# Turning the normalized x by transposing DMAs instead of TensorE, in an attention and spectral kernel

## The chip, the cores and the metric

The kernel runs on one core of a Trainium2 chip. The metric is the time of one execution in device microseconds (us); of several executions the median is given.

## The reference, cut to what matters

Two layers, each an attention block and a spectral filter, both on a layernorm of x and both added to x. S is 2048 tokens, D is 1024 columns, there are 32 heads of 32 columns.

```python
def _A_ref(x, wqkv, wo):                      # attention
    qkv = (x @ wqkv).reshape(B, S, 3, H, Dh).transpose(2, 0, 3, 1, 4)
    q, k, v = qkv[0], qkv[1], qkv[2]
    p = softmax(einsum("bhqd,bhkd->bhqk", q, k) * Dh ** -0.5)
    return einsum("bhqk,bhkd->bhqd", p, v).transpose(0, 2, 1, 3).reshape(B, S, D) @ wo
def _B_ref(x, w_r, w_i):                      # spectral filter
    return irfft2(rfft2(x) * (w_r + 1j * w_i))

x = x + _A_ref(layernorm(x), wqkv, wo)
x = x + _B_ref(layernorm(x), w_r, w_i)
...                                           # the same two lines once more
```

## The kernel before

The tokens are cut into 16 tiles of 128, the chunks of a query or key sum have 512 tokens (four tiles, `NCH` = 4), and the heads go in 8 groups of four (`NG`). x stays in on-chip memory (`ap.x`). The products with the weights are done in float16 pairs: a number is split into a high float16 part (ScalarE, ACT in the profile) and a low one, the rest (VectorE, DVE), by `split` (L167, L168); three matmuls, high by high, high by low and low by high, make one product.

Each layer's attention begins with a **prologue**, which makes everything that the first group of heads needs:

- `ln_tile(t)` normalizes a token tile: two statistics on DVE (`bn_stats`, L111, L112; in layer 1 half of those of the first six tiles are made earlier), small instructions on DVE and one on GpSimd (L119 to L124, L302), then one ACT instruction that writes the normalized tile `xn` in float32 (L304). In layer 0 it also starts the load of the x tile four places on (L293).
- `tr_tile(t, xn)` turns it, so that columns lie on partitions: eight TensorE transposes with an identity matrix into PSUM (L310), and then `split` from PSUM into `xh` and `xl`, views of the big buffer (named big in the profile).
- `v_tiles(ph, t2)` makes V for two token tiles, 48 matmuls of 256 columns (L372), eight times.
- `qk_chunk(ph, c)` makes a chunk of K or Q, 24 matmuls of 512 columns (L328), four times for K and four times for Q. Its split goes to ACT and DVE, and its squares to GpSimd (L332), for `norms` and `mkbias` (L345 to L358), which yield the bias of the first Exp.
- `prep` loads a weight piece by SP and splits it (L248 to L258); in layer 1 this was done earlier, beside the spectral stage.

`xn` comes from a pool with the tag "p", which has eight slots of 4 KB a partition. The attention's K, Q and V are written over x tiles that have been normalized (R in the profile is that buffer).

Behind the prologue comes the main loop over groups, query chunks and key tiles (scores L548, Exp L552, sums with V L558, row sums L571), whose TensorE and ACT order is written out by hand, with the weights' products of later groups put between. In the prologue no order is written out: there the framework orders the instructions of each engine, by the place in the program and by its own estimates of when an operand is ready. It also places all semaphores. Each engine and each DMA queue then works its list in order. Nearly all DMAs are issued by SP, one queue.

Between the two attentions stands the spectral stage of layer 0. At its end the sixteen tiles of the new x are stored to memory by SP (L982, 512 KB each), in the program ahead of layer 1's prologue.

Of the kernel before, what the change touches and what calls it, by code (L numbers as in the profile page):

```python
# [6 lines left out]
F32 = mybir.dt.float32  # L7
F32R = mybir.dt.float32r
F16 = mybir.dt.float16
# [91 lines left out]
SX = 2.0 ** 8  # L101
# [7 lines left out]
def bn_stats(nc, sm, x):  # L109
    st = sm.tile([128, 2, 6], F32, name="st")  # L110
    nc.vector.bn_stats(st[:, 0], x[:, 0:512])  # L111
    nc.vector.bn_stats(st[:, 1], x[:, 512:1024])  # L112
    return st
# [14 lines left out]
def ln_stats(nc, sm, cst, st, mv):  # L128

    nc.vector.bn_aggr(mv, st)  # L130
    return ln_scale(nc, sm, cst, mv, nc.vector)
# [33 lines left out]
def split(nc, hi, lo, src, scale):  # L165

    nc.scalar.activation(hi, src, AF.Copy, scale=scale)  # L167
    nc.vector.scalar_tensor_tensor(lo, src, scale, hi, op0=ALU.mult, op1=ALU.subtract)  # L168


def run(g):
    for _ in g:
        pass
# [52 lines left out]
class Weights:  # L226
# [5 lines left out]
    def prep(self, ph):  # L232
        nc, ap, wp = self.nc, self.ap, self.wp
        kind, g = ph
        if kind == "v":
            w = self.W[ph] = ap.wvp.tile([128, 2, 8, 256], F16, name="wv")
            sl = [(w[:, 0, 4 * j:4 * j + 4, 128 * i:128 * i + 128], w[:, 1, 4 * j:4 * j + 4, 128 * i:128 * i + 128],
                   wp[g + i, 2, :, 512 * j:512 * j + 512]) for i in range(2) for j in range(2)]
        else:
            w = self.W[ph] = ap.wqp.tile([128, 2, 8, 128], F16, name="wqk")  # L240
            sl = [(w[:, 0, 4 * j:4 * j + 4], w[:, 1, 4 * j:4 * j + 4],
                   wp[g, 0 if kind == "q" else 1, :, 512 * j:512 * j + 512]) for j in range(2)]
        st = []

        def load():
            if len(st) < len(sl):
                s = ap.sgp.tile([128, 4, 128], F32, name="wst")
                nc.sync.dma_start(s, sl[len(st)][2].rearrange("p (d c) -> p d c", c=128))  # L248
                st.append(s)
        for _ in range(3):  # L250
            load()
        yield
        for i, (h, l, _) in enumerate(sl):
            split(nc, h, l, st[i], SW)
            if self.flag is not None:
                wm = ap.sm.tile([128, 1], F32, name="wm")
                nc.vector.tensor_reduce(wm, st[i], axis=AX.XY, op=ALU.max, apply_absolute_value=True)
                nc.vector.tensor_max(self.flag, self.flag, wm)  # L258
            load()
            yield  # L260
# [3 lines left out]
PH0 = [("v", 0), ("k", 0), ("q", 0)]  # L264


def attention(nc, tc, layer, ap, xin, yd, wts, wo, cst, dram, flags):

    ident = cst["ident"]
    W, prep = wts.W, wts.prep  # L270
    od = dram.tile([2, NG, 128, 2048], F16, name=f"od{layer}")
    small, psum = ap.small, Pools(tc, None)
    pp, qp, sgp, wqp, wvp = ap.pp, ap.qp, ap.sgp, ap.wqp, ap.wvp
    sq, on, on2, sm = ap.sq, ap.on, ap.on2, ap.sm
    psS = psum("at_psS", 3, space=PSUM)
# [4 lines left out]
    def bank():  # L280

        if both:
            both.append(True)
            if len(both) % 2:
                return psO.tile([128, 512], F32, name="o")
        return psX.tile([128, 512], F32, name="x")
    xhl = ap.big.bitcast(F16).rearrange("p (c a d n) -> p c a d n", a=2, d=8, n=512)
    xh, xl = ([xhl[:, c, a] for c in range(4)] for a in range(2))
    V, K, Q, bias, nrm, mx = {}, {}, {}, {}, {}, {}

    def ln_tile(t):
        if layer == 0 and t + 4 < 16:
            nc.sync.dma_start(ap.x[:, t + 4], xin[(t + 4) * 128:(t + 5) * 128, :])  # L293
        mv = flags["mv"][:, layer * 16 + t]
        if layer and t < NST:
            st = flags["st"][:, t]
            nc.vector.bn_stats(st[:, 1], ap.x[:, t, 512:1024])
        else:
            st = bn_stats(nc, sm, ap.x[:, t])
        r = ln_stats(nc, sm, cst, st, mv)  # L300
        b = sm.tile([128, 1], F32, name="b")
        nc.vector.scalar_tensor_tensor(b, mv[:, 0:1], -1.0, r, op0=ALU.mult, op1=ALU.mult)  # L302
        xn = pp.tile([128, 1024], F32, name="xn", tag="p")
        nc.scalar.activation(xn, ap.x[:, t], AF.Identity, bias=b, scale=r)  # L304
        return xn

    def tr_tile(t, xn):
        pt = psS.tile([128, 8, 128], F32, name="s")
        for d in range(8):
            nc.tensor.transpose(pt[:, d], xn[:, d * 128:(d + 1) * 128], ident)  # L310
        c, o = t // 4, (t % 4) * 128
        split(nc, xh[c][:, :, o:o + 128], xl[c][:, :, o:o + 128], pt, SX)

    def qk_chunk(ph, c):
        kind, g = ph
        w = W[ph]
        if c == 0:
            if kind == "k":
                K[g] = ap.k[g % 3]
            else:  # L320
                Q[g] = qp.tile([128, 2, 2048], F16, name="Q") if g % 2 else ap.q
            p_, n_ = (qp, "Q") if ph == ("q", 0) else (sq, "sq")
            nrm[ph] = p_.tile([128, 4, 512], BF16, name="sq", tag=n_)
        t = (K if kind == "k" else Q)[g][:, :, c * 512:c * 512 + 512]
        ps = bank()
        for d in range(8):
            for i, (a, b) in enumerate(((w[:, 0, d], xh[c][:, d]), (w[:, 0, d], xl[c][:, d]), (w[:, 1, d], xh[c][:, d]))):
                nc.tensor.matmul(ps, a, b, start=d == 0 and i == 0, stop=d == 7 and i == 2)  # L328
                if d < 7 or i < 2:
                    yield  # L330
        split(nc, t[:, 0], t[:, 1], ps, SQ / (SX * SW))
        nc.gpsimd.tensor_tensor(nrm[ph][:, c], t[:, 0], t[:, 0], op=ALU.mult)  # L332
        if c == 3:
            left_norms.append(ph)
        yield
# [3 lines left out]
    def norms():  # L339
        kind, g = ph = left_norms.pop(0)  # L340
        if g not in mx:
            mx[g] = sm.tile([128, 2], F32, name="mqk")
        ps = psS.tile([128, 2, 512], F32, name="s")
        for c in range(4):
            nc.tensor.matmul(ps[32 * c:32 * c + 32, 0], cst["bones"], nrm[ph][:, c], start=True, stop=True)  # L345
        i = 0 if kind == "k" else 1
        nc.vector.reduce_max(mx[g][:, i:i + 1], ps[:, 0], axis=AX.X)
        if kind == "q":
            mkbias(g)

    def mkbias(g):
        r = sm.tile([128, 2], F32, name="mall")
        nc.gpsimd.partition_all_reduce(r, mx[g], 128, bass.bass_isa.ReduceOp.max)
        b = sm.tile([128, 1], F32, name="bpr")
        nc.gpsimd.tensor_tensor(b, r[:, 0:1], r[:, 1:2], op=ALU.mult)
        nc.gpsimd.tensor_tensor(b, b, cst["half"], op=ALU.pow)
        bias[g] = sm.tile([128, 1], F32, name="bias")
        nc.gpsimd.tensor_scalar(bias[g], b, -SCALE / (SQ * SQ), None, op0=ALU.mult)  # L358
# [142 lines left out]


    vk = [v_tiles(PH0[0], t) for t in range(8)]
    xn = [ln_tile(0), ln_tile(1)]
    if not layer:
        run(prep(PH0[0]))

    def ln_to(t):
        while len(xn) <= min(t, 15):
            xn.append(ln_tile(len(xn)))  # L510
    for t in range(4):
        tr_tile(t, xn[t])
        ln_to(t + 2)
        if not layer and t in (1, 2):
            run(prep(PH0[t]))
        if t % 2:
            run(vk.pop(0))
    ln_to(7)
    for c in range(NCH):
        t = 4 * c + 4  # L520
        run(qk_chunk(PH0[1], c))
        if t < 16:
            tr_tile(t, xn[t])
            ln_to(t + 3)
        run(qk_chunk(PH0[2], c))
        if t < 16:
            for i in range(1, 4):
                tr_tile(t + i, xn[t + i])
                ln_to(t + i + 3)
                if i == 2:  # L530
                    run(vk.pop(0))
        elif c == 3:
            norms()
            norms()
    for v in vk:
        run(v)
    both.clear()
# [77 lines left out]
    with tc.manual_schedule(engines={mybir.EngineType.PE, mybir.EngineType.Activation}):  # L615
        for g in range(NG):
# [3 lines left out]
            for u in range(NCH * NKT):  # L620
                c, kt = divmod(u, NKT)
# [25 lines left out]
                elif g == NG - 1:  # L647
                    t = rests[0] if rests else 16
# [472 lines left out]
def build(nc, tc, a):  # L1121
    with ExitStack() as ctx:
# [29 lines left out]
        for layer in range(2):  # L1152
            y = dr.tile([2048, 1024], F32, name=f"y{layer}")
            attention(nc, tc, layer, ap, x, y, wts[layer], a["wo"], cst, dr, flags)
            x = a["out"] if layer else x1
            if layer:
                spectral(nc, tc, ap, y, x, a, cst, True)
            else:
                spectral(nc, tc, ap, y, x, a, cst, True, flags, (s for ph in PH0 for s in wts[1].prep(ph)))
# [39 lines left out]
```

## Time and profile before

| | |
|---|---|
| median of 3 runs | 3951.18 us (3951.08 to 3956.0) |
| the profiled execution | 3952.66 us |
| its span, first to last instruction | 3950.8 us |
| TensorE busy | 95% |
| DVE busy | 82% |
| ACT busy | 73% |
| GpSimd busy | 16% |
| mean granted TensorE clock | 0.985 of full speed |

In the rows of the profile, a group is a line, an engine, an operation, output<-input, shapes and a count, then busy time and the mean of one in ns, then idle time of the engine just before and what ended it. PE is TensorE's matmuls, PEld its weight loads, POOL is GpSimd, SPq is the issue of a DMA on SP. A timeline row begins with start and duration in us. Matmuls overlap in the pipeline, so the duration of one is longer than the distance between two.

### The profile page before, as it was taken

How to read it: one execution, taken by the hardware profiler on the slowest of the kernel's cores; microseconds unless marked ns; L12 is line 12 of the kernel's file. 1: busy time of each engine (PE TensorE's matmuls, PEld its weight loads, DVE VectorE, ACT ScalarE, POOL GpSimd, SP SyncE). 2: the span in 40 equal slices, each digit the busy share in tenths (PEclk: the TensorE clock that was granted, in tenths of full speed). 3: DMA queues.
4: the chain of work that ended last, by engine and by line, in shares of the span. 5: the costliest groups of instructions: out<-in, count | busy, mean ns of one | idle time of the engine just before them, and what ended most of it. 6: DMA issues, size and time to landing. Idle time of an engine off the chain costs nothing.

```text
span 3950.8 us, 80100 instructions
## 1 busy us (share of the span) xinstructions
PE 3770.9 (95%) x33204; PEld 1671.8 (42%) x33204; DVE 3225.5 (82%) x3845; ACT 2893.9 (73%) x3565; POOL 643.4 (16%) x591
## 2 busy tenths in 40 slices
PE   7999999999999999989989999999999999999898
PEld 5322432342243233378854334333422432333787
DVE  6699888989998978866765998899899888788456
ACT  4587887888788766658745888888888887665585
POOL 1011011101110200014321220122021111000143
PEclk9999999999999999999999999999999999999999
DMA  3000000000000211143120000000000002122323
GB/s 116 14 15 19 12 12 17 17 14 19 12 23 12 89 52 68 54 177 108 55 86 12 15 23 12 12 17 24 8 17 17 17 12 89 57 73 83 120 94 102
DMA packets 97559, 177.31 MB, mean 45 GB/s; under 512 B 7200, under 2 KB 52896, under 8 KB 96160
## 3 DMA queue, kind: packets, MB, share of 16 engines
q1 hardware_dynamic: 97040, 172.03, 12.7%
q8 instruction: 262, 4.29, 0.4%
q14 instruction: 113, 0.93, 0.1%
q10 hardware_dynamic: 144, 0.07, 0.0%
HBM read 123.83 MB, written 48.23 MB: 44 GB/s over the span
## 4 chain that ended last, share of the span: by engine, by line
PE 76%; DVE 9%; issue 7%; ACT 4%; POOL 3%; DMA 1%; SPq 0%; DVEq 0%; ACTq 0%; POOLq 0%
PE o L558 21%; PE s L548 17%; PE x L328 13%; PE x L372 8%; PE x L431 6%; DVE R L571 2%; ACT p L552 2%; PE ps L833 2%; PE ps L771 2%; PE s L577 1%; PE o L372 1%; PE ps L762 1%; PE ps L948 1%; PE o L328 1%; PE ps L902 1%
## 5 line engine op out<-in xcount | busy, mean ns | idle before, releaser
L552 ACT ACTIVATE p<-s,bias 128x1024 f32<-128x1024 f32 x2048 | 2168.3, 1111 | 585.0 <-PE s L548 573.8
L571 DVE TENSOR_TENSOR R<-R,p 128x1024 f32<-128x1024 f32 x1792 | 2145.8, 1250 | 142.2 <-ACT p L552 138.1
L558 PE MATMUL o<-p,R 128*32 128x512 f32 x8192 | 985.0, 598 | 0.0
L328 PE MATMUL x<-big,wqk 128*128 128x512 f16 x2880 | 686.6, 384 | 22.7 <-DVE R L168 8.2
L548 PEld LDWEIGHTS <-R 32*128 32x128 f16 x12288 | 231.1, 92 | 781.1 <-issue 664.8
L328 PEld LDWEIGHTS <-wqk 128*128 128x128 f16 x3072 | 277.6, 98 | 460.7 <-issue 169.4
L548 PE MATMUL s<-R 32*128 32x512 f16 x6144 | 431.9, 379 | 19.0 <-ACT p L552 15.5
L548 PE MATMUL s<-Q,R 32*128 32x512 f16 x6144 | 432.0, 378 | 11.9 <-ACT p L552 10.6
L558 PEld LDWEIGHTS o<-p,R 128*32 128x32 f32 x8192 | 213.7, 109 | 523.5 <-issue 522.9
L591 POOL TENSOR_TENSOR ohl<-zt,ohl 128x512 f16<-128x512 f32 x62 | 180.0, 2903 | 1473.4 <-ACT ohl L590 1473.4
L372 PEld LDWEIGHTS <-big 128*128 128x128 f16 x3072 | 293.3, 99 | 117.2 <-issue 69.8
L372 PE MATMUL x<-wv,big 128*128 128x256 f16 x2688 | 323.5, 277 | 12.5 <-DVE R L168 6.0
L569 DVE SCALAR_TENSOR_TENSOR R<-p 128x1024 f32<-128x1024 f32 x128 | 153.8, 1203 | 197.5 <-ACT p L552 197.1
L332 POOL TENSOR_TENSOR sq<-R 128x512 bf16<-128x512 f16 x96 | 142.4, 1483 | 703.0 <-ACT R L167 702.5
L431 PE MATMUL x<-big 128*128 128x512 f16 x1008 | 228.0, 380 | 0.0
L431 PEld LDWEIGHTS <-big 128*128 128x128 f16 x1344 | 126.8, 98 | 177.9 <-issue 35.8
L881 DVE TENSOR_TENSOR H<-G,H 128x512 f16<-128x512 f32 (+1 forms) x68 | 46.8, 688 | 106.1 <-ACT H L880 105.9
L833 PE MATMUL ps<-cbi,H 128*128 128x256 f16 (+1 forms) x792 | 99.1, 273 | 6.2 <-ACT H L880 4.3
L826 ACT COPY U<-ps 64x256 f32<-64x256 f32 (+1 forms) x272 | 97.0, 357 | 7.9 <-PE ps L833 2.7
L826 ACT COPY B<-ps 64x256 f32<-64x256 f32 (+1 forms) x272 | 97.0, 356 | 6.7 <-PE ps L833 2.4
L332 POOL TENSOR_TENSOR sq<-Q 128x512 bf16<-128x512 f16 x32 | 45.1, 1409 | 321.3 <-ACT Q L167 321.3
L833 PE MATMUL ps<-cb,big 128*128 128x256 f16 x780 | 96.3, 273 | 0.0
(418 smaller groups left out, 3145.0 us busy)
## 6 DMA issues: line engine op xcount, KB each, us to landing
wst<-in_wp SPq DMA_DIRECT2D x96, 256.0 KB, 3.0
R<-y SPq DMA_DIRECT2D x32, 512.0 KB, 5.2
w<-in_w SPq DMA_DIRECT2D x60, 256.0 KB, 2.6
od<-ohl SPq DMA_DIRECT2D x56, 256.0 KB, 2.4
big<-od SPq DMA_DIRECT2D x16, 896.0 KB, 7.1
y<-R SPq DMA_DIRECT2D x20, 512.0 KB, 2.6
R<-in_x SPq DMA_DIRECT2D x16, 512.0 KB, 6.6
wst<-in_wo SPq DMA_DIRECT2D x32, 256.0 KB, 3.0
```

The source lines that it names most:

```text
L328: nc.tensor.matmul(ps, a, b, start=d == 0 and i == 0, stop=d == 7 and i == 2)
L332: nc.gpsimd.tensor_tensor(nrm[ph][:, c], t[:, 0], t[:, 0], op=ALU.mult)
L372: nc.tensor.matmul(ps[:, j], l, r, start=d == 0 and i == 0, stop=d == 7 and i == 2)
L431: nc.tensor.matmul(p, a, b, start=start and d == ds[0] and i == 0, stop=stop and d == ds[-1] and i == 2)
L548: nc.tensor.matmul(s[h // 2][:, h % 2], K[g][r, a, kt * 128:kt * 128 + 128], Q[g][r, b, c * 512:c * 512 + 512], start=i == 0, stop=i == 2)
L552: nc.scalar.activation(p, s[hf], AF.Exp, bias=bias[g], scale=SCALE / (SQ * SQ))
L558: nc.tensor.matmul(O[g, c][32 * h:32 * h + 32], V[g][:, kt, 32 * h:32 * h + 32], P[g, c, kt, h // 2][:, h % 2], start=kt == 0, stop=kt == ...
L569: nc.vector.scalar_tensor_tensor(acc[hf], P[g, c, 0, hf], 1e-34, p, op0=ALU.add, op1=ALU.add)
L571: nc.vector.tensor_add(acc[hf], acc[hf], p)
L591: eng.tensor_tensor(t[:, 1], r, t[:, 0], op=ALU.subtract)
L826: nc.scalar.copy(ov[64 * r:64 * r + 64, a0:a0 + m, x], tl[64 * x:64 * x + 64, :m, r])
L833: nc.tensor.matmul(out, l, r, start=k == 0, stop=k == len(mm_) - 1)
```

## The change

`tr_tile` is gone. `ln_tile` does all of it: it splits the normalized tile in its token layout, from on-chip memory, into a tile `hl` of the same pool "p" (two halves, high and low), and two transposing DMAs on SP turn the halves into `xh` and `xl`. The order of the calls in the program is written anew: two tiles are normalized ahead of each K or Q chunk, a V sum follows each of the first three chunks of K and Q, and the rest of V comes last, as before.

```diff
-    ident = cst["ident"]
...
         xn = pp.tile([128, 1024], F32, name="xn", tag="p")
         nc.scalar.activation(xn, ap.x[:, t], AF.Identity, bias=b, scale=r)
-        return xn
-
-    def tr_tile(t, xn):
-        pt = psS.tile([128, 8, 128], F32, name="s")
-        for d in range(8):
-            nc.tensor.transpose(pt[:, d], xn[:, d * 128:(d + 1) * 128], ident)
+        hl = pp.tile([128, 2, 1024], F16, name="hl", tag="p")
+        split(nc, hl[:, 0], hl[:, 1], xn, SX)
         c, o = t // 4, (t % 4) * 128
-        split(nc, xh[c][:, :, o:o + 128], xl[c][:, :, o:o + 128], pt, SX)
+        for i, p in enumerate((xh, xl)):
+            nc.sync.dma_start(p[c][:, :, o:o + 128], hl[:, i], transpose=True)
...
     vk = [v_tiles(PH0[0], t) for t in range(8)]
-    xn = [ln_tile(0), ln_tile(1)]
+    ln_tile(0)
+    ln_tile(1)
     if not layer:
         run(prep(PH0[0]))
-
-    def ln_to(t):
-        while len(xn) <= min(t, 15):
-            xn.append(ln_tile(len(xn)))
-    for t in range(4):
-        tr_tile(t, xn[t])
-        ln_to(t + 2)
-        if not layer and t in (1, 2):
-            run(prep(PH0[t]))
-        if t % 2:
-            run(vk.pop(0))
-    ln_to(7)
+    ln_tile(2)
+    ln_tile(3)
+    run(vk.pop(0))
+    if not layer:
+        run(prep(PH0[1]))
+    ln_tile(4)
+    ln_tile(5)
+    run(vk.pop(0))
+    if not layer:
+        run(prep(PH0[2]))
     for c in range(NCH):
-        t = 4 * c + 4
-        run(qk_chunk(PH0[1], c))
-        if t < 16:
-            tr_tile(t, xn[t])
-            ln_to(t + 3)
-        run(qk_chunk(PH0[2], c))
-        if t < 16:
-            for i in range(1, 4):
-                tr_tile(t + i, xn[t + i])
-                ln_to(t + i + 3)
-                if i == 2:
-                    run(vk.pop(0))
-        elif c == 3:
+        for i, ph in enumerate(PH0[1:]):
+            for t in range(4 * c + 6 + 2 * i, min(4 * c + 8 + 2 * i, 16)):
+                ln_tile(t)
+            run(qk_chunk(ph, c))
+        if c == 3:
             norms()
             norms()
+        else:
+            run(vk.pop(0))
     for v in vk:
         run(v)
```

## The prediction

> **What bounds the kernel now.** I began with the head of the profile page, then cut the two attention prologues out of the trace, because the change touches nothing else: in windows of 20 us (columns: PE, PEld, DVE, ACT and POOL busy with instruction counts, granted clock, DMA share, GB/s).
>
> ```profile
> span 3950.8 us, 80100 instructions
> PE 3770.9 (95%) x33204; PEld 1671.8 (42%) x33204; DVE 3225.5 (82%) x3845; ACT 2893.9 (73%) x3565; POOL 643.4 (16%) x591
> ```
> ```profile
> 0.00:20.00 20.00, 5.08 (x24) 4.10 (x25) 15.61 (x55) 8.37 (x10) 2.42 (x8) 0.96 0.77 294
> 20.00:40.00 20.00, 18.39 (x135) 13.77 (x134) 19.32 (x78) 12.60 (x16) 3.28 (x6) 0.95 0.74 274
> 40.00:60.00 20.00, 16.86 (x104) 11.92 (x103) 16.38 (x63) 12.69 (x15) 5.30 (x8) 0.83 0.01 1
> 60.00:80.00 20.00, 19.81 (x135) 13.51 (x134) 6.19 (x6) 7.41 (x10) 2.08 (x2) 1.00 0.00 1
> ```
>
> The whole span is TensorE's (95%), and so is the prologue of layer 0, but only from 60 us on (19.81 of 20). Ahead of that DVE is busy with the normalization (15.61, 19.32 and 16.38 us of each 20) and TensorE has holes. The DMA engines are at about three quarters in the first 40 us and then idle. A prologue ends where the first score matmul (L548) starts. The timeline of layer 0 gives the ends of it:
>
> ```profile
> 10.60 2.37 ACT L304 ACTIVATE xn<-R,b,r 128x1024 f32<-128x1024 f32 x2 [4.56 <-DVE b L302]
> 18.93 6.60 PE L372 MATMUL x<-wv,big 128*128 128x256 f16 x46 [1.46 <-DVE big L168]
> 20.07 0.68 DVE L168 SCALAR_TENSOR_TENSOR wv<-wst,wv 128x512 f16<-128x512 f32 x1
> 128.06 1.03 PE L548 MATMUL s<-R 32*128 32x512 f16 x14
> ```
>
> and those of layer 1, with the sixteen stores of x1 on SP:
>
> ```profile
> 1993.54 18.17 SPq L982 DMA_DIRECT2D x<-R  x16
> 2000.91 3.68 PE L310 MATMUL s<-ident,xn 128*128 128x128 f32 x16 [15.43 <-ACT xn L304]
> 2006.11 5.20 PE L372 MATMUL x<-wv,big 128*128 128x256 f16 x46 [0.33 <-DVE b L302]
> 2107.20 1.04 PE L548 MATMUL s<-R 32*128 32x512 f16 x14
> ```
>
> So the prologues last to 128.06 us, and to 2107.20 us with the first V sum at 2006.11.
>
> **What is removed.** The groups of TensorE instructions in the window of layer 0's prologue, and then of layer 1's (the last column is idle time before them and who ended it):
>
> ```profile
> L372 PE MATMUL x<-wv,big 128*128 128x256 f16 x192 | 26.0, 300 | 6.2 <-DVE big L168 2.9 <-ACT big L167 1.7 <-DVE wv L168 1.4
> L328 PE MATMUL x<-big,wqk 128*128 128x512 f16 x96 | 22.0, 379 | 1.4 <-ACT big L167 1.4
> L328 PE MATMUL o<-big,wqk 128*128 128x512 f16 x96 | 21.9, 379 | 1.4 <-DVE big L168 0.9 <-ACT big L167 0.6
> L310 PE MATMUL s<-ident,xn 128*128 128x128 f32 x128 | 17.9, 296 | 11.9 <-ACT xn L304 11.9
> L345 PE MATMUL s<-sq,bones 128*32 128x512 bf16 x8 | 1.4, 384 | 0.3 <-POOL sq L332 0.3
> ```
> ```profile
> L372 PE MATMUL o<-wv,big 128*128 128x256 f16 x192 | 22.0, 273 | 1.7 <-DVE big L168 1.5 <-ACT big L167 0.2
> L328 PE MATMUL o<-big,wqk 128*128 128x512 f16 x96 | 21.8, 379 | 1.3 <-DVE big L168 0.7 <-ACT big L167 0.6
> L310 PE MATMUL s<-ident,xn 128*128 128x128 f32 x128 | 17.8, 292 | 15.5 <-ACT xn L304 15.4
> ```
>
> Gone are 128 transposes a layer: 17.9 and 17.8 us, 0.14 us each, 1.1 us a tile. Those of tiles 0 and 1 lie ahead of the first V sum, so of each layer some 14 x 1.1 = 15.7 us are on TensorE's path behind it. Gone too are the waits of TensorE for the split of a turned tile (big, by ACT and DVE): in layer 0 2.9 + 1.7 + 1.4 + 0.9 + 0.6 = 7.5 us, in layer 1 1.7 + 1.3 = 3.0 us. What stays is the sums themselves. Two pieces of the chain that ended last, and the group L345 above, size them:
>
> ```profile
> 73.20 5.24 PE o L372 x48
> 81.68 5.12 PE x L328 x23
> ```
>
> Eight V sums by 5.24 and eight q or k sums by 5.12 are 82.9 us; with the norms' 1.4 + 0.3 it is 84.6 us of TensorE a layer, which no edit here can shorten.
>
> **What stays on ACT and DVE.** Both halves of a split now read SBUF, not PSUM. The same operations in this window, turned tile against staged weights:
>
> ```profile
> L304 ACT ACTIVATE xn<-R,b,r 128x1024 f32<-128x1024 f32 x16 | 19.7, 1239 | 16.6 <-DVE b L302 16.4
> L167 ACT ACTIVATE big<-s 128x1024 f16<-128x1024 f32 x16 | 15.9, 1017 | 2.3 <-PE s L310 2.3
> ```
> ```profile
> L168 DVE SCALAR_TENSOR_TENSOR big<-s,big 128x1024 f16<-128x1024 f32 x10 | 12.0, 1217 | 3.7 <-ACT big L167 3.7
> L111 DVE BATCH_NORM_STATS2 st<-R 128x6 f32<-128x512 f32 x16 | 10.9, 680 | 3.3 <-DMA R<-in_x 3.3
> L124 DVE TENSOR_TENSOR r<-r,n 128x1 f32<-128x1 f32 x16 | 2.3, 146 | 0.1
> L257 DVE TENSOR_REDUCE wm<-wst 128x1 f32<-128x512 f32 x11 | 7.3, 675 | 0.0
> L168 DVE SCALAR_TENSOR_TENSOR wv<-wst,wv 128x512 f16<-128x512 f32 x4 | 2.7, 681 | 0.0
> ```
>
> ACT's half rises from 1.02 to about the 1.24 of xn, which also reads SBUF: 16 x 0.22 = 3.5 us a layer on an engine busy 12.7 of 20 at most; costed at nothing while ACT keeps that room, 3.5 us if it has none. DVE's half on SBUF takes 0.68 for 512 columns, so for 1024 about the 1.22 of before (at most twice 0.68). DVE therefore does what it did, but in the order that tiles need it: the low half of tile t comes right behind its statistics. Two statistics (1.36), the low half (1.22) and seven small instructions (0.15 each, 1.1) are 3.7 us a tile, an upper bound because their ends overlap. The statistics begin at 4.7 us, when x lands; four tiles and the V and K weights (six pieces of eleven, each with a reduction and a low half of 0.68, 1.3 in all) end at 4.7 + 14.8 + 7.8 = 27 us.
>
> **What is added: 32 transposing DMAs of 256 KB a layer, all on SP.** No such DMA is in this trace. The nearest rows, DMA issues by size and time to landing, and the DMA share around the end of the stores:
>
> ```profile
> wst<-in_wp SPq DMA_DIRECT2D x96, 256.0 KB, 3.0
> x<-R SPq DMA_DIRECT2D x16, 512.0 KB, 5.5
> mm<-in_mm_ SPq DMA_DIRECT2D x2, 128.0 KB, 2.3
> ```
> ```profile
> 2000.00:2001.00 1.00, 0.09 (x1) 0.09 (x2) 1.00 (x5) 0.86 (x1) 0.07 (x1) 0.50 1.05 414
> 2005.00:2006.00 1.00, 0.67 (x5) 0.42 (x4) 1.00 (x2) 0.98 (x2) 0.55 (x1) 1.00 1.02 406
> 2010.00:2015.00 5.00, 4.12 (x35) 3.35 (x33) 4.76 (x21) 4.82 (x8) 1.10 (x2) 1.00 1.03 404
> 2015.00:2020.00 5.00, 4.19 (x39) 3.75 (x40) 5.00 (x18) 2.58 (x4) 1.10 (x2) 1.00 0.04 15
> ```
>
> Let T be the time that one transposing DMA takes of the queue when others stand behind it. The lower end is the plain stream: sixteen stores of 512 KB in 18.17 us of issue are 1.14 us each, so 0.57 us for 256 KB. The upper end is a whole landing, 3.0 us, if no transfer overlaps the next. I take 1.1 us, twice the plain stream, nearer to that end because the rows show DMAs of this size streaming through one queue; and 3 us from issue to landing when alone.
>
> Two pages of the Trainium skill speak for the lower end. Its "Advanced Engine Details and Errata", section "X-Bar Transpose (TRN2)", holds transposing DMAs to be as fast as plain ones. "DMA: Bandwidth & Descriptors", section "Latency and other measured facts", has 261 GB/s measured, by which T would be an estimated 1.0 us, and the sum below would not move.
>
> *Layer 0.* xn of tiles 0 and 1 is there at 12.97 us; two high and two low halves and a landing bring the turned tiles to about 20 us, and the last V weight piece is split at 20.75 anyway. So the first V sum starts near 21 rather than 18.93, at half clock at first, as it did (192 matmuls took 26.0 us where 192 of layer 1 took 22.0; there were two slow spells, the granted clock fell again in the 40 to 60 us row: I add 2 us for one). It ends at 28; the next needs tile 3, at 27 + 3 = 30. From there 84.6 - 5.2 = 79.4 us of TensorE follow without a turn between: 109.4, and with about 1.5 us for gaps the scores start at 111, 17 us earlier. DVE could set a later end: all sixteen tiles, 4.7 + 59.2 + 14.3 for eleven weight pieces + 3 for the q and k splits + 3 landing = 84 us, behind which the last k and q, the norms and three V sums take 27.7 us: 112. With overlapped DVE ends it is less. So 109 to 113. On SP a transpose waits for its low half, and the x loads of later tiles and weights stand behind it; DVE waits for those. x comes four tiles ahead, 15 us at DVE's pace; costed at nothing, and if that cover were gone a landing of 3.0 us would show for each load.
>
> *Layer 1.* Here SP is not free. The sixteen stores come first in program order and are ready first; they are issued until 1993.54 + 18.17 = 2011.7, and fill the DMA engines (404 GB/s) until about 2015. Before, TensorE turned tiles 0 and 1 beside them. Now the first four transposes stand behind 8 MB: 2015 + 4 x 1.1 + 2.4 (a landing less its 0.6 of stream) = 2021.8 is the start of the first V sum, not 2006.11. TensorE then has been idle since the stage before, and the clock in the rows above is 0.50 from the first matmul for about 4 us, which now falls on the V sum: 2 us. 2021.8 + 84.6 + 2 = 2108.4: 1 us later than before. What 128 transposes give back, the stores take. If the first tiles land at the stream's 0.57 and 1 us of latency it is 2103; if they land 4 us later, 2112. Slots for xn and its halves (eight, two a tile) hold seven tiles by then; DVE is not held up much.
>
> **The sum.** -17 + 1 = -16 us against the profiled execution's 3952.66 us: 3936.7. That execution lies 1.5 us over the median of 3951.18, so I put the median of the changed kernel at 3935 us; with the ends given, 3927 to 3945. About 0.2% (8 us) is what a measurement of this kernel can tell from no change.
>
> **Rivals.** *The transposes follow one another at landing time.* Then the DMA queue is the bound. Layer 0: first issue at 13 us, last tile at 13 + 32 T + 2, and 27.7 us behind: 42.7 + 32 T. Layer 1: 2015 + 32 T + 2 + 27.7 = 2044.7 + 32 T. They cross the old ends at T = 2.67 and 1.95 us, together at 2.3 us, from which on the kernel is slower. At T = 3.0 they end at 138.7 and 2140.7: +10.6 + 33.5 = 44 us, 3995. For it: nothing in the trace shows a transfer from SBUF to SBUF, let alone a turning one; against it: every other 256 KB stream overlaps. 0.18.
>
> *Each DMA is turned block by block*, eight blocks of 128x128, each like a small transfer. The nearest is 128 KB in 2.3 us; at that T is 18.4 us, and 64 x 18.4 - 148 = +1030 us (148 is 64 times the joint crossing of 2.3): 4980. In part overlapped it would be some hundreds. 0.12. The Trainium skill, "VectorE: DVE Perf Modes", section "The three transpose paths", has 1309 ns for a 128x128 block by DMA against 390 ns by TensorE; at eight blocks in a row T would be an estimated 10.5 us and the time near 4475. This trace's 0.14 us a block for TensorE in a row is well under that page's figure for it, so its figures look like single blocks, not streams.
>
> *The scheduler moves V sums ahead of the last k and q.* Rows of the end of layer 0's prologue:
>
> ```profile
> 106.08 5.13 PE L328 MATMUL x<-big,wqk 128*128 128x512 f16 x23
> 127.25 0.27 POOL L358 TENSOR_SCALAR bias<-bpr 128x1 f32<-128x1 f32 x1
> ```
>
> From the last q sum's end (111.2) to the bias that the first Exp needs (127.5) are 16.3 us, hidden under three V sums. With two of them drawn ahead, 10.5 us a layer lie bare: -16 + 21 = +5, 3956, no change to be told. 0.07. Against it: in the trace of before the bias had the time of three V sums, as the program's order has it.
>
> **How the numbers follow.** Forecast 0.57; serial queue 0.18; blocks 0.12; reordering 0.07; 0.06 is left for what I can't name, half of it faster. Faster 0.60, same 0.07, slower 0.33. The range reaches over the reordering and the serial queue to 3.1 us a DMA: 3926 to 4000; blocks and half of the rest stay out.
>
> **What would show it.** Right: no L310 group; 32 transposes a layer landing within about 4 us where the queue is free; the score matmuls at about 111 us, and in layer 1 about 93 us after the last store has landed; TensorE's idle time in layer 1 before the first V sum about 36 us, ended by a DMA. Wrong: TensorE waiting for big by DMA between sums beyond chunk 0, or a DMA share high until the prologue's end (serial); the first V sum of layer 1 at about 2006 (the stores didn't hold the transposes, and it is 15 us faster than I say); Exp idle for POOL's bias (reordering).

## The result, and the profile after

The changed kernel takes 3955.94 us (median of 12 runs, 3953.41 to 3959.05) where the kernel before, timed beside it, takes 3954.91 us (12 runs, 3949.21 to 3960.05). The ratio is 1.0004, interval 0.9995 to 1.0013: no change that 0.2% can tell. 16 us less were forecast. The profiled execution took 3958.61 us, its span is 3956.7 us, its mean granted clock 0.982.

The head of the page of the changed kernel:

```profile
span 3956.7 us, 79721 instructions
PE 3744.6 (95%) x32948; PEld 1642.1 (42%) x32948; DVE 3224.8 (82%) x3845; ACT 2894.7 (73%) x3565; POOL 653.2 (17%) x591
```

TensorE lost 256 matmuls, as the edit says, and 26.3 us of busy time (3770.9 before), and yet the span did not shrink. Now the timeline of layer 0's prologue, SP, DVE and TensorE together (V sums are L368 here, q and k sums L324, scores L537, the transposing DMAs L308, weight loads L248, x loads L292):

```profile
12.90 4.05 SPq L308 DMA_TRANSPOSE big<-hl  x2
17.67 3.34 SPq L308 DMA_TRANSPOSE big<-hl  x2
21.07 1.54 SPq L248 DMA_DIRECT2D wst<-in_wp  x3
...
27.42 6.39 PE L368 MATMUL x<-wv,big 128*128 128x256 f16 x35 [1.42 <-DVE wv L168]
33.64 5.40 PE L368 MATMUL o<-wv,big 128*128 128x256 f16 x48
...
57.42 9.51 SPq L308 DMA_TRANSPOSE big<-hl  x5
66.97 0.58 SPq L248 DMA_DIRECT2D wst<-in_wp  x1
...
70.51 0.69 DVE L257 TENSOR_REDUCE wm<-wst 128x1 f32<-128x512 f32 x1 [5.36 <-DMA wst<-in_wp]
73.27 0.68 DVE L168 SCALAR_TENSOR_TENSOR R<-o,R 128x512 f16<-128x512 f32 x1
74.00 6.73 PE L368 MATMUL o<-wv,big 128*128 128x256 f16 x48 [7.65 <-DVE R L168]
...
123.97 1.03 PE L537 MATMUL s<-R 32*128 32x512 f16 x14
```

Read from the bottom. The scores start at 123.97, 4.1 us earlier than before (128.06), not 17. At 74.00 TensorE had been idle for 7.65 us, for a low half of an earlier sum on DVE (73.27). DVE, which takes its list in order, had stood still for 5.36 us ahead of its reduction of a weight piece, and that piece was issued by SP only at 66.97, behind five transposes that began at 57.42. SP did not wait for a half of a tile there: from 47.52 to 66.93 it issued ten transposes with one x load between them, without a pause, 1.87 us each, and the halves of tiles 9 to 11 had been ready for 3.5 to 5.8 us when their transposes left (single issues, not shown). At the start it is the same: the last weight piece of the first V sum was issued at 21.07, behind the transposes of tiles 0 and 1, and TensorE waited for its split until 27.42. Neither wait is for a turned tile; TensorE waits for weights that stand behind transposes. TensorE's waits in the first 140 us say it too (in total, times, longest; of the 20.3 us 16.6 lie ahead of its first matmul):

```profile
PE x L368 <- ACT wv L167: 20.3, 2, 16.6
PE o L368 <- DVE R L168: 7.7, 1, 7.7
PE x L368 <- DVE wv L168: 3.9, 2, 2.5
```

Windows (columns as in the prediction) of layer 0, then of layer 1 with the stores alone and with the transposes:

```profile
20.00:40.00 20.00, 14.88 (x100) 11.08 (x98) 15.97 (x51) 12.17 (x16) 2.63 (x4) 1.00 1.05 245
60.00:80.00 20.00, 12.35 (x73) 7.57 (x72) 11.79 (x36) 10.34 (x12) 3.69 (x5) 0.83 1.12 200
1995.00:2010.00 15.00, 0.00 (x0) 0.00 (x0) 13.80 (x54) 8.87 (x8) 4.34 (x6) 0.50 1.02 404
2020.00:2060.00 40.00, 35.46 (x226) 22.58 (x225) 24.10 (x71) 23.18 (x27) 9.52 (x10) 0.97 1.06 183
```

From 60 to 80 us, where TensorE had been busy for 19.81 of 20 us, it is now busy for 12.35, and the DMA engines, idle there before, are full. In layer 1 the DMA share is full at 404 GB/s with plain stores and just as full at 183 GB/s with transposes. The timeline of layer 1:

```profile
1993.97 18.14 SPq L971 DMA_DIRECT2D x<-R  x16
2012.22 48.04 SPq L308 DMA_TRANSPOSE big<-hl  x32
2017.96 0.60 PE L368 MATMUL x<-wv,big 128*128 128x256 f16 x2 [32.04 <-DMA big<-hl]
2019.14 6.75 PE L368 MATMUL x<-wv,big 128*128 128x256 f16 x46 [0.57 <-DMA big<-hl]
2033.52 5.34 PE L324 MATMUL x<-big,wqk 128*128 128x512 f16 x24 [2.40 <-ACT R L372]
2046.35 5.40 PE L368 MATMUL x<-wv,big 128*128 128x256 f16 x48 [1.56 <-DVE R L168]
2110.59 1.04 PE L537 MATMUL s<-R 32*128 32x512 f16 x14
```

The first transpose is issued when the sixteenth store is, TensorE is idle for 32.0 + 0.6 us ahead of the first V sum (15.4 before), and the scores start 116.62 us after the first store, where it was 2107.20 - 1993.54 = 113.66 us: 3.0 us later. So the first prologue gained 4.1 and the second lost 3.0.

Two marks therefore serve for every kernel below: the start of layer 0's first score matmul, and layer 1's, counted from the first store of x1. Where kernels have the same code in a layer their marks differ by up to 1.8 us in layer 0 (119.04 and 120.83) and 3.0 us in layer 1 (116.33 to 119.28). So the size of the loss in layer 1 is uncertain; its sign is not, for the three kernels with the changed code there lie 2.7 to 5.6 us above the two with the old (113.66 and 113.68).

### The profile page after: what moved, and what is told of

Read it like the earlier page. It is cut to its first block, busy times and chain, and to the rows that moved or that the text cites. A ratio compares the mean times of both kernels' runs of the same rounds, so it can differ in the third digit from the quotient of the medians.

```text
span 3956.7 us, 79721 instructions
## 1 busy us (share of the span) xinstructions
PE 3744.6 (95%) x32948; PEld 1642.1 (42%) x32948; DVE 3224.8 (82%) x3845; ACT 2894.7 (73%) x3565; POOL 653.2 (17%) x591
## 5 line engine op out<-in xcount | busy, mean ns | idle before, releaser
L324 PE MATMUL x<-big,wqk 128*128 128x512 f16 x2880 | 691.1, 386 | 23.7 <-DVE R L168 8.7
L537 PEld LDWEIGHTS <-R 32*128 32x128 f16 x12288 | 231.1, 92 | 781.9 <-issue 665.9
L324 PEld LDWEIGHTS <-wqk 128*128 128x128 f16 x3072 | 278.8, 99 | 466.5 <-issue 175.7
L537 PE MATMUL s<-R 32*128 32x512 f16 x6144 | 432.5, 379 | 19.8 <-ACT p L541 16.3
L537 PE MATMUL s<-Q,R 32*128 32x512 f16 x6144 | 432.4, 378 | 11.3 <-ACT p L541 10.6
L368 PE MATMUL x<-wv,big 128*128 128x256 f16 x2688 | 325.8, 278 | 64.4 <-DMA big<-hl 32.6
L368 PEld LDWEIGHTS <-big 128*128 128x128 f16 x3072 | 295.3, 99 | 176.6 <-issue 86.5
```

Of the source, the lines that this page charges most:

```text
L368: nc.tensor.matmul(ps[:, j], l, r, start=d == 0 and i == 0, stop=d == 7 and i == 2)
L537: nc.tensor.matmul(s[h // 2][:, h % 2], K[g][r, a, kt * 128:kt * 128 + 128], Q[g][r, b, c * 512:c * 512 + 512], start=i == 0, stop=i == 2)
```

## The experiments

The theory, A in the expectations: SP issues in order; a transpose waits on SP for its low half, so every load behind it waits too (weights and x in layer 0), and in layer 1 the transposes themselves wait behind the stores; TensorE starts late, and what its transposes gave back goes into idle time. The trace above agrees at the start, but near 60 us it is the transposes' own time on the queue, not a wait for a half, that holds the loads. The rivals carry other letters, each stated where it is tested. Ratios are to the kernel before on the same chip, with 95% intervals; the marks are in us.

| kernel | layer 0 | layer 1 | ratio |
|---|---|---|---|
| before | 128.06 | 113.66 | 1 |
| changed | 123.97 | 116.62 | 1.0004 (0.9995 to 1.0013) |
| weights_act | 120.03 | 116.33 | 0.9988 (0.9979 to 0.9997) |
| before_weights_act | 131.84 | 113.68 | 1.0014 (1.0005 to 1.0023) |
| weights_early | 120.83 | 119.28 | 0.9993 (0.9984 to 1.0002) |
| stores_behind | 123.08 | 107.91 | 0.9979 (0.9969 to 0.9989) |
| weights_and_stores | 119.30 | 106.46 | 0.9964 (0.9950 to 0.9978) |
| early_and_stores | 119.04 | 107.79 | 0.9959 (0.9946 to 0.9972) |
| transposes_doubled | 123.97 | 141.37 | one execution, +23.5 us |
| first_four_by_tensor | 111.77 | 102.43 | 0.9924 (0.9911 to 0.9936) |
| last_four_by_tensor | 123.87 | 118.43 | 1.0010 (1.0000 to 1.0020) |
| all_by_tensor | 121.67 | 109.09 | 0.9974 (0.9964 to 0.9983) |
| first_eight_by_tensor | 115.03 | 106.48 | 0.9949 (0.9932 to 0.9965) |
| first_four_and_early | 109.46 | 102.43 | 0.9933 (0.9919 to 0.9947) |

The two marks carry the time: their joint shift against before agrees with the measured one to 4 us in every row. first_four moves them by 16.3 + 11.2 = 27.5 us, measured 0.0076 x 3955 = 30; transposes_doubled by -4.1 + 27.7 = +23.6, measured +23.5; all_by_tensor by 6.4 + 4.6 = 11.0, measured 0.0026 x 3958 = 10. What the main loops and the spectral stage add lies within those 4 us.

**weights_act**: the weight pieces of layer 0's prologue, and those of the next group's first sum, are issued by ACT, not by SP.

```diff
-                nc.sync.dma_start(s, sl[len(st)][2].rearrange("p (d c) -> p d c", c=128))
+                q.dma_start(s, sl[len(st)][2].rearrange("p (d c) -> p d c", c=128))   # q = nc.scalar in layer 0's prologue
```

> The changed kernel, with the weight pieces of layer 0's prologue issued from ACT's queue, so that none stands behind a transpose on SP. Theory A (in layer 0 the weight pieces that stand on SP behind transposes cost the gain: the fourth V piece issued at 21.07 us, a K piece for the next group at 66.97): the first V sum is done by about 28 us instead of 33.8, the 7.65 us wait of TensorE at 66 us is gone, and the first score matmul comes at about 112 us instead of 123.97; the time falls by about 12 us against the changed kernel. Rival B (the DMA engines, at a share of 1.05 from 20 to 80 us, are themselves the bound, whichever queue issues): the first score matmul stays at 120 us or later.

The mark came to 120.03, which is what rival B had named (120 or later), and the long wait near 70 us shrank to 1.58 us. The start became worse in another way, as its timeline shows:

```profile
19.78 5.65 SPq L309 DMA_TRANSPOSE big<-hl  x3
23.10 0.61 PE L369 MATMUL x<-wv,big 128*128 128x256 f16 x2 [23.10 <-DMA big<-hl]
71.39 5.40 PE L369 MATMUL o<-wv,big 128*128 128x256 f16 x48 [1.58 <-DVE R L168]
```

ACT works in order as well, and now waited for weight pieces ahead of its part of tile 0: the first transpose left at 19.78 instead of 12.90, and the second V sum was done at 44 us instead of 39. From there to the mark it took 76 us, where the changed kernel took 85 and the forecast had 79.4 - 5.2 + 1.5 = 76. In that stretch DVE waited for no load any more, neither for a weight piece (5.36 us in the changed kernel) nor for x (0.93), and TensorE for no DMA, though the DMA share was 1.00 to 1.13 from 20 to 80 us, as full as in the changed kernel. So the later half of theory A is seen, and full DMA engines by themselves don't hold that stretch, as rival B has it. Its size is not: TensorE came 5 us later, which hides as much of a wait for DVE, so of the 9 us saved some 4 are surely the loads'. For the start the run shows nothing, because the edit brought a wait of its own.

**before_weights_act**: the same edit in the kernel before, for the rival that weights off SP's queue help whatever turns the tiles.

> The kernel before, with the weight pieces of its layer 0's prologue on ACT's queue: does that edit help without transposing DMAs too? Theory A: there TensorE waited 1.4 us for a V weight piece and DVE bounds the first 60 us, so 0 to 3 us. Rival C (the weights' queue is a fault of both kernels and has nothing to do with the transposes): as much as weights_act against the changed kernel, 10 us or more.

Layer 0's mark went from 128.06 to 131.84, layer 1's stayed (113.68), and the ratio is 1.0014. ACT's queue costs 3.8 us by itself; the rival falls.

**weights_early**: the eight weight pieces of layer 0's prologue are loaded by SP into buffers that are idle there, ahead of the first transpose.

```diff
+    if not layer:
+        wts.early()          # eight loads on SP, of V, K and Q
     ln_tile(0)
     ln_tile(1)
```

> The changed kernel, with all eight weight pieces of layer 0's prologue loaded on SP ahead of the first transpose, into buffers that are idle then (those of the main loop's outputs). ACT's order is left alone, unlike in weights_act. Theory A (weight pieces behind transposes on SP): no wait of TensorE for a weight piece or behind the reduction of one; the first V sum is done by about 28 us, the first score matmul comes at 110 to 113 us instead of 123.97, 11 to 14 us less. Rival B (the DMA engines are full from 20 to 80 us, weights, x and transposes only trade places): 118 us or later; then TensorE waits for big by DMA.

```profile
19.63 7.68 PE L382 MATMUL x<-wv,big 128*128 128x256 f16 x46 [1.32 <-DMA big<-hl]
30.98 6.86 PE L382 MATMUL o<-wv,big 128*128 128x256 f16 x46 [2.03 <-DMA big<-hl]
67.41 5.40 PE L382 MATMUL o<-wv,big 128*128 128x256 f16 x48 [3.61 <-DVE n L123]
70.88 0.57 SPq L262 DMA_DIRECT2D wst<-in_wp  x1
74.20 0.69 DVE L271 TENSOR_REDUCE wm<-wst 128x1 f32<-128x512 f32 x1 [3.68 <-DMA wst<-in_wp]
75.73 7.03 PE L338 MATMUL x<-big,wqk 128*128 128x512 f16 x24 [2.92 <-DVE R L168]
```

The first V sum was done at 27.3 instead of 33.8, as expected: the weights behind the transposes were what held it. (The edit also spares the fourth V piece its wait for one of three staging buffers; in the changed kernel the first of them was free at 16.96, not shown, 4 us before that piece was issued, so most of the delay is the transposes'.) The mark was not: 120.83 instead of 110 to 113, which is what rival B had named (118 or later), and its sign came too, for TensorE waited 1.32, 1.24 (not shown) and 2.03 us for turned tiles. Against the forecast's 111 the rows give 2.5 us at the second V sum, done at 37.7 instead of 35.2, for tiles turned late; 3.61 us ahead of 67.41, where DVE was behind with its list, after an x load behind a transpose had held it for 1.47 us (not shown); 2.92 us ahead of 75.73, where DVE had stood still for 3.68 us, because the next group's weight piece, which this edit does not move, was issued at 70.88 behind later transposes; and 1.7 us of slow sum there (7.03 us for 5.34). So this run shows theory A for the first V sum alone. What came in its place is the same queue at later places, and how much of that is its order and how much its rate, this run does not separate.

**stores_behind**: ten of the sixteen stores of x1 are issued between the transposes, two tiles behind.

```diff
             nc.sync.dma_start(p[c][:, :, o:o + 128], hl[:, i], transpose=True)
+        if layer:
+            for u in (6 + t - 2,) if t < 15 else range(6 + t - 2, 16):
+                if 6 <= u < 16:
+                    nc.sync.dma_start(xin[u * 128:(u + 1) * 128, :], ap.x[:, u])
...
-        for t in range(16):
+        for t in range(6):
```

> The changed kernel, with ten of the sixteen stores of x1 issued one by one behind the transposes of layer 1's prologue, not all ahead of them. Theory A (the stores ahead on SP delay the first V sum of layer 1): it starts at about 2009 us instead of 2019, the first score matmul at about 2101 instead of 2110.6; 9 to 10 us less than the changed kernel. Rival B (transposes, at 1.5 us each with full DMA engines, and stores together need 48 + 20 us of the DMA engines, so the order changes nothing): the first score matmul stays within 3 us of 2110.6.

```profile
1990.54 5.33 SPq L975 DMA_DIRECT2D x<-R  x6
1998.97 8.98 SPq L308 DMA_TRANSPOSE big<-hl  x6
2004.58 6.93 PE L372 MATMUL x<-wv,big 128*128 128x256 f16 x46 [1.88 <-DMA big<-hl]
2036.69 8.10 PE L328 MATMUL o<-big,wqk 128*128 128x512 f16 x24 [3.45 <-DVE R L168]
2098.45 1.03 PE L541 MATMUL s<-R 32*128 32x512 f16 x14
```

The first V sum starts 14.0 us after the first store, not 25.2, and the scores at 107.9, 8.7 earlier: the stores ahead of the transposes were layer 1's loss. Some came back as a wait for DVE (3.45 us) and for a store (0.72 us, not shown).

**weights_and_stores** and **early_and_stores** put two edits together.

> Both edits together. Theory A: the gains add, the first score matmuls at about 112 us and, counted from the first store of x1, 107 us later (116.6 before the edit): 20 to 22 us less than the changed kernel, about as much below the kernel before, 3930 to 3935. Rival B: less than 8 us.

> weights_early and stores_behind together, all tiles turned by DMA. Theory A: the gains add, 110 to 113 us in layer 0 and about 108 us after the first store in layer 1: 20 to 23 us less than the changed kernel. Rival B: 9 to 13 us less, the stores' part alone.

They are faster than before by 0.36% and 0.41%, some 16 to 18 us under the changed kernel by the ratios, less than the 20 to 23 expected, for what their first edits lacked in layer 0 (119.30 and 119.04).

**transposes_doubled**: each transposing DMA of layer 1 is issued once more, into an idle buffer.

```diff
             nc.sync.dma_start(p[c][:, :, o:o + 128], hl[:, i], transpose=True)
+            if layer:
+                nc.sync.dma_start(on2.tile([128, 8, 128], F16, name="ohl"), hl[:, i], transpose=True)
```

> The changed kernel, with every transposing DMA of layer 1 issued once more into an idle buffer, whose content nothing reads. If one takes 1.5 us of the DMA engines and the prologue's end is the last tile's landing and 27.7 us behind it, the first score matmul comes 18.2 + 64 x 1.5 + 2 + 27.7 = 144 us after the first store of x1. If SP's issue is what takes 1.5 us and the engines are not full, the same; if TensorE stays the bound, at most 120 us.

```profile
2102.32 1.35 SPq L310 DMA_TRANSPOSE ohl<-hl  x1
2133.67 1.04 PE L539 MATMUL s<-R 32*128 32x512 f16 x14
2060.00:2100.00 40.00, 31.40 (x186) 18.12 (x183) 5.12 (x6) 7.47 (x13) 4.16 (x4) 0.96 1.08 183
```

From 2010.60 to 2103.67 are 64 issues, 1.45 us each; the scores came 141.4 us after the first store (144 by the formula of the rival of the serial queue at this T). With 32 of them (48.04 us, 1.50 each) the queue ends at 2060.3, far ahead of the last V sums, so its rate is not what sets layer 1's end in the changed kernel. With 64 it is.

**first_four_by_tensor**: tiles 0 to 3 of each layer are turned by TensorE as before, the other twelve by DMA.

```diff
+        if t < 4:
+            pt = psS.tile([128, 8, 128], F32, name="s")
+            for d in range(8):
+                nc.tensor.transpose(pt[:, d], xn[:, d * 128:(d + 1) * 128], cst["ident"])
+            c, o = t // 4, (t % 4) * 128
+            split(nc, xh[c][:, :, o:o + 128], xl[c][:, :, o:o + 128], pt, SX)
+            return
         hl = pp.tile([128, 2, 1024], F16, name="hl", tag="p")
```

> The changed kernel, but tiles 0 to 3 of each layer are turned by TensorE as before, tiles 4 to 15 by DMA. Theory A (what the change loses is lost at the start of each prologue, before the first four tiles are there): the first V sums start as before, at about 19 us and 12 to 13 us after the first store of x1; the first score matmuls at about 111 us and 101 to 103 us after that store (116.6 in the changed kernel, 113.7 before); about 26 us less than the changed kernel, 24 us less than the one before. Rival B (the DMA engines are the bound): the first V sums come early, but later sums wait for big by DMA, and the gain is under 15 us.

It took 3926.84 us (3925.93 to 3929.03): 0.9924, faster than both kernels. Its timeline:

```profile
18.15 6.02 PE L375 MATMUL x<-wv,big 128*128 128x256 f16 x41 [0.77 <-DVE big L168]
111.77 1.04 PE L544 MATMUL s<-R 32*128 32x512 f16 x14
1981.51 18.66 SPq L978 DMA_DIRECT2D x<-R  x16
1996.36 4.09 PE L375 MATMUL x<-wv,big 128*128 128x256 f16 x36
2000.28 38.38 SPq L315 DMA_TRANSPOSE big<-hl  x24
2083.94 1.03 PE L544 MATMUL s<-R 32*128 32x512 f16 x14
```

The first V sum starts at 18.15, and in layer 1 while the stores still run; the transposes from 2000.28 on lie under sums that need only the first four tiles. TensorE waits for no turned tile by DMA.

**last_four_by_tensor**, its control: tiles 12 to 15 by TensorE (`t >= 12`), so there is as much of either kind, and the start is that of the changed kernel.

> The control for first_four_by_tensor: as many tiles of each layer turned by TensorE (four) and by DMA (twelve), but the last four by TensorE, so the start is that of the changed kernel. Theory A (what counts is who turns the first tiles): the first score matmul of layer 0 stays at 121 to 126 us, that of layer 1 at 113 to 119 us after the first store, and the time within 6 us of the changed kernel's, a ratio of 0.998 to 1.002. Rival B (first_four was faster because there is less transposing traffic): 112 and 102 us as in first_four, a ratio near 0.992.

```profile
27.63 5.75 PE L375 MATMUL x<-wv,big 128*128 128x256 f16 x35 [1.42 <-DVE wv L168]
2022.45 6.26 PE L375 MATMUL x<-wv,big 128*128 128x256 f16 x46 [0.61 <-DMA big<-hl]
```

123.87 and 118.43, ratio 1.0010, as the changed kernel. What counts is who turns the first tiles, not how many go by DMA: by the ratios 34 us lie between these two kernels. That layer 0's mark is the changed kernel's to 0.1 us is in part chance: the start is the same, but the wait of 7.65 us is gone, and four tiles' transposes and 4.0 us of waiting for their xn stand in its place.

**all_by_tensor**: all sixteen by TensorE (`t < 16`), in the changed kernel's new program order.

> All sixteen tiles by TensorE from PSUM, as before, but in the program order of the changed kernel, so the rewritten order alone is tried. Theory A (the order is nearly neutral): the first score matmul of layer 0 at 125 to 131 us, that of layer 1 at 112 to 117 us after the first store, a ratio of 0.998 to 1.003. Rival D (the new order is itself bad and hides what the DMAs gain): 10 us or more a layer later, a ratio over 1.004. Rival E (first_four got its time from the new order, not from the DMAs): 112 and 102 us, a ratio near 0.993.

Not foreseen, by any of the three theories: 0.9974, 10 us faster than before by the order alone. The groups of TensorE in layer 0's prologue, and two rows of layer 1's timeline:

```profile
L375 PE MATMUL x<-wv,big 128*128 128x256 f16 x192 | 25.3, 294 | 2.1 <-DVE wv L168 1.3 <-DVE big L168 0.8
L331 PE MATMUL o<-big,wqk 128*128 128x512 f16 x96 | 21.5, 379 | 0.0
L307 PE MATMUL s<-ident,xn 128*128 128x128 f32 x128 | 18.0, 294 | 13.2 <-ACT xn L303 13.2
```
```profile
1991.93 18.13 SPq L978 DMA_DIRECT2D x<-R  x16
2101.02 1.03 PE L544 MATMUL s<-R 32*128 32x512 f16 x14
```

TensorE turns all its tiles (18.0 us) and still nearly all waits for big are gone: 0.8 is left on the first group, where it was 2.9 + 1.7, the 1.4 us of the second are 0.0, and 1.0 lies on the other V group (not shown), where it was 0.2. The new order did that. Rival D falls, and so does E: the order alone gives 121.67 and 109.09, not the 111.77 and 102.43 of first_four. Against this kernel the transposing DMAs alone make the changed one later by 2.3 us in layer 0, little over the spread there, and 7.5 in layer 1.

**first_eight_by_tensor**: `t < 8`.

> As first_four_by_tensor with eight tiles by TensorE. Theory A: the start is already covered by four, so four tiles more cost their transposes, 4 x 1.1 us a layer, and nothing else: first scores at about 116 us and 107 us after the first store, 8 to 10 us over first_four, a ratio of 0.994 to 0.996. Rival F (the DMA engines are still what holds the prologue with four): fewer DMAs give as much as the transposes cost or more, a ratio of 0.992 or less.

115.03 and 106.48, 3.3 and 4.1 us later than with four, for transposes of 4.4 us; the time is 0.9949. With four the DMAs are covered already.

**first_four_and_early**: four by TensorE, and the early weight loads.

> The first four tiles of each layer by TensorE, the rest by DMA, and the eight weight pieces of layer 0's prologue loaded ahead of the first transpose as in weights_early. Theory A: with the first four tiles by TensorE no weight piece of the first sums stands behind a transpose any more, so what is left for the early loads is the 1.3 us that the first V sum waits for its last weight piece and the 0.5 to 2 us behind it: layer 0's first score matmul at 109 to 112 us, layer 1 as in first_four (102.4 us after the first store), 0 to 3 us under first_four, a ratio of 0.991 to 0.993. Rival G (the weight loads on SP are still a cost of their own in the hybrid): 5 us or more under first_four, a ratio of 0.991 or less.

Layer 0's mark is 2.3 us earlier (109.46), layer 1's the same, and the ratio, 0.9933 (0.9919 to 0.9947, another chip), can't be told from first_four's. No weight load is a great cost in the hybrid; the simpler first_four stays the best version.

## Why the prediction was wrong

**What failed: "x loads of later tiles and weights stand behind it ... costed at nothing".** The working named the queue, but the cover that it gave, four tiles ahead, is that of the x loads; it did not look where the *weight* loads stand, and it took the split of the last V piece, 20.75, over from the kernel before, where no transpose is on the queue. In the changed kernel that piece was issued at 21.07 and split at 27.4. From 111 to 123.97 are 13 us, in two parts. The first V sum was done at 33.8 instead of 28, and so the second started at 33.6, where 30 was said for tile 3: 3.6 us. From there to the scores it took 90.3 us instead of 79.4 + 1.5: the wait of 7.65 us, 1.5 us in smaller ones, and 1.5 us because the V sum behind the long wait took 6.73 us instead of 5.24, for 1.5 us given. weights_early shows that the first V sum was held by its weights (done at 27.3), and weights_act that DVE's wait, and some 4 us of the second part, go when the loads are off that queue. No run has both, and the best all-DMA mark in layer 0 is 119.04, so 111 was not reached without turning the first tiles by TensorE. The stated price, 3.0 us a load if the cover were gone, was the landing; the true price was the landing and the transposes ahead of it, through DVE in order, to TensorE.

**What was mis-sized: T.** 1.1 us was taken between 0.57 and 3.0; it is 48.04 / 32 = 1.50. It stays under the crossing at 2.3, so the rival of the serial queue did not happen, and in layer 1 this cost nothing by itself. In layer 0 it has a part in what failed. An estimate: DVE finished the low halves of tiles 6 to 11 at 3.0 us a tile (from 45.35 to 60.44, not shown). At 1.1 us a transpose and 0.57 for an x load the queue needs 2.8 us a tile and keeps up; at the 19.4 us that it took for five tiles from 47.52 to 66.93 it needs 3.9 and falls behind, and the weight piece with it. The DMA share of 1.05 to 1.12 from 20 to 80 us is the trace of that. No run changed T alone. By the Trainium skill, "Advanced Engine Details and Errata", section "X-Bar Transpose (TRN2)", transposing DMAs are as fast as plain ones. The trace disagrees: 183 GB/s here against 404 at equally full engines.

**Layer 1: right in its mechanism, and 2 us off because two errors nearly cancel.** The first V sum was said to start at 2021.8 and started at 2019.14; the scores were said to come 1 us later than before and came 3.0 later. From the start of the first V sum it took 91.5 us instead of 86.6: waits of 2.40, 1.56 and two smaller ones, for ACT and DVE, which were normalizing and splitting tiles when the sums' results came. For these waits the sum had nothing. ACT's half itself was dearer in the forecast (1.24) than it is (1.05, the mean of 16).

**What the sum did not separate.** The forecast credited the DMAs with the waits for big, 7.5 and 3.0 us. all_by_tensor shows that the new order takes most of them with TensorE kept: 10 us, where 16 were forecast, were to be had without any DMA. Then the DMAs take 9.8 us away by the marks, though they free TensorE of 18.0 us of transposes in layer 0 and 17.5 in layer 1.

**What held.** No L310 group; 32 issues a layer; landing 3.1 us at least and 3.4 at the median (7.3 at most, above the 4 said); TensorE's idle time before layer 1's first V sum 32.6 us for the 36 said, ended by a DMA; 0.63 us of waiting for big by DMA beyond that. Its signs of the serial queue came only in part: that one wait beyond chunk 0 was short, and layer 0's DMA share stayed full until 80 us, not until the prologue's end; what TensorE waited long for was not big. The measured time lies on the 3956 us that the rival of the reordering had named, but by chance: the last three V sums still come behind the last q sum, as in the kernel before.

## What to carry to other kernels

DMAs of computed operands, on a queue that works in order, delay every load behind them, by waiting for the operand or by their own time on the queue: for each moved step list what its queue holds next, weights as well as data, and price each by the wait ahead of it, not by its own landing. Work taken from an engine is worth something only where that engine can start; at a stage's start, where TensorE is idle anyway, its own transposes are the quickest way to the first operand, and DMAs serve for the later tiles (first four by TensorE: 0.9924; last four: 1.0010). When an edit also rewrites the program order, try the order alone: here it was worth 10 us, and the DMAs took as much away again.

## What the runs showed of the hardware that was not expected

Fed one behind the other, transposing DMAs of 256 KB take 1.45 to 1.50 us each, whether 32 or 64 of them, at full DMA engines and 183 GB/s, under half of what the same engines move in plain stores (404). One that SP issues after 3 us of idleness still holds SP two to three times as long as a plain one of 512 KB (L292) does, by these rows of the changed kernel's SP:

```profile
33.33 0.43 SPq L292 DMA_DIRECT2D R<-in_x  x1
36.74 1.24 SPq L308 DMA_TRANSPOSE big<-hl  x1
46.80 0.61 SPq L292 DMA_DIRECT2D R<-in_x  x1
```

In layer 0, with one x load among them, ten in a row took 1.87 us each. Whether the issue (1.24 us) or the engines set the 1.45 to 1.50 us was not separated. Transposes from two queues at once were not tried.
